# GpSimd takes the short operations behind every four expert dots and behind their tanh

## The chip, the cores and the metric

The kernel runs on one core of a Trainium2 chip. The metric is the device time of one execution in microseconds; the comparison rests on medians of several runs. The core's engines are TensorE (PE, with its weight load PEld), VectorE (DVE), ScalarE (ACT), GpSimd (POOL) and SyncE (SP, which here only issues DMAs). Each runs its own instructions in order and waits on semaphores for the others.

## The reference, cut to what matters

Input x is 2048 rows of 512 floats. After a layer norm, the output is the sum of x, an attention and a layer of many small experts:

```python
xn = _layernorm(x, axis=-1)
return x + _A_ref(xn, ...) + _B_ref(xn, ...)
# _A_ref: 32 heads of 16, one shared k and v: softmax(q k^T / 4) v, then @ wo
# _B_ref, for every row and each of 32 heads:
#   s1, s2 = q1 @ k1^T, q2 @ k2^T          64 scores each
#   the best 2 of each, the best 2 of their 4 sums -> 2 experts of 4096, gates g = softmax
act = _gelu(jnp.einsum("nd,nhkd->nhk", xf, u[top_e]))
out = jnp.einsum("nhk,nhk,nhkd->nd", g, act, v[top_e])
```

The gelu is the tanh form: half of a (1 + tanh(0.798 a + 0.0357 a^3)).

## The kernel before, in words

The 2048 rows are 16 tiles of 128, in four groups of four. Two ways of computing the experts stand side by side.

**Gathered experts** serve the first eight tiles (`ph` 0 and 1), for the first of the heads' chosen experts at a time: a slot is one expert for each of a tile's 128 rows. There are 512 slots. For every slot, `gather` (L969) has POOL fetch 128 rows of u and v side by side with an indirect DMA into one of 12 buffers; `dot` (L981) multiplies the u half with xn and sums it on DVE into one column of a 128x4 tile `act`; `add` (L1014) adds the v half, times its weight, to the tile's total on DVE and so frees the buffer. Between dot and add, four slots together (a group, 128 in all) pass through short operations on 128x4 tiles: L997 and L998 form the argument of the tanh (`q`, then `y`), L999 multiplies the dots with the gates (`ga`), ACT takes the tanh (`tanh`, L1002, row L1004), and L1011 in `weigh` makes the weight `w = (th + 1) ga`. All four but the tanh are on DVE.

**Dense experts** serve the other eight tiles, in two stages (`dense`, L656): gates are spread over all 4096 experts with one-hot matmuls (`pg`, L815), then u and v run as plain matmuls in blocks of 128 experts (`pact` L733, `pout` L861), with DVE splitting operands (L698, L919), multiplying gates (L904, L907, L924) and adding totals (L864).

Ahead of both, `item` (L512) scores one tile against a share of the heads with 12 matmuls into a PSUM buffer `psc` (L531); DVE finds the best eight and their places (L544, L546); after every four items `batch` (L563) does the choice of the best two, with part of it on POOL (L590 to L606 for the gathered, L590 to L638 for the dense experts).

Attention runs through all of this in 256 double steps (`att_steps`, L1142): scores (`sc`, L326), exp on ACT (`pt`, L329), times v (`pv`, L340). One PE item of other work fills each step: `fill` runs scores or dense work up to a planned time.

The order of the instructions on every engine is written out by hand (`manual_schedule`, L1248): each engine runs what the program emits for it, in the order of emission. In a step, `mid` (L1264) emits first the tanhs of the groups whose dots stand in earlier steps, then this step's dots, with `weigh` ahead of the last dot, and then `go` (L1294): one add, one operation of `CHAIN`, one of `BEHIND` in turn, and up to four gathers. `CHAIN` is the list into which `dot` puts L997 to L999, so that these lie between adds; in the one-hot stages (`dense_on` 2) the whole list runs right after the dots. The three PSUM buffers of the tag `x` serve psc, pact, pout, pg and the small transposes in turn; DVE or ACT frees them. The tiles of the short operations rotate over three or four buffers.

Of the kernel before, what the change touches and what calls it, by code (L numbers as in the profile page):

```python
# [11 lines left out]
F32 = mybir.dt.float32  # L12
# [5 lines left out]
AF = mybir.ActivationFunctionType  # L18
OP = mybir.AluOpType
# [4 lines left out]
P = 128  # L24
# [15 lines left out]
SB = 4  # L40
# [7 lines left out]
C_IN = 0.7978845608028654  # L48
C_CUB = 0.044715 * C_IN
# [6 lines left out]
def tile_kernel(ctx, tc, x, wq, wkv, wo, wqT, kT, uv, ub, vb, out):  # L56
    nc = tc.nc
# [6 lines left out]
    small = pool("small", bufs=2)  # L64
# [381 lines left out]
    def experts_out(t):  # L446
        acc, last = ACC[t], t // GT == QB[3]
        assert last or t in DONE_A
        store(lambda: nc.sync.dma_start(d_part[t] if last else out[t * P:(t + 1) * P, :], acc))
        LIVE.discard(t)  # L450
# [513 lines left out]
             for h in range(NEG // 2) for k in range(2) for i in range(2)]  # L964
    NSL = len(slots)
    UV, WT, ACTS, TH, GA = {}, {}, {}, {}, {}
    CHAIN = []

    def gather(m):  # L969
        ph, c, ti, s = slots[m]  # L970
# [10 lines left out]
    def dot(m):  # L981
        ph, c, ti, s = slots[m]
        n, i = divmod(m, SB)
        if i == 0:
            ACTS[n] = small.tile([P, SB], F32, name="act", bufs=3)
        a = ACTS[n]
        u = UV[m][:, :D]
        nc.vector.tensor_tensor_reduce(u, u, XN[TPH * ph + ti], scale=1.0, scalar=0.0,  # L988
                                       op0=OP.mult, op1=OP.add, accum_out=a[:, i:i + 1])
        if i == SB - 1:  # L990
            q = small.tile([P, SB], F32, name="gq", bufs=3)
            y = small.tile([P, SB], F32, name="gy", bufs=3)
            ga = small.tile([P, SB], F32, name="ga", bufs=4)
            gg = G[ph, c][:, ti - 1:ti + 1, s // 2, :].rearrange("p t k -> p k t")
            pairs = lambda v: v.rearrange("p (k t) -> p k t", t=2)
            stt = nc.vector.scalar_tensor_tensor
            CHAIN.append(lambda: stt(q, a, C_CUB, a, op0=OP.mult, op1=OP.mult))  # L997
            CHAIN.append(lambda: stt(y, q, C_IN, a, op0=OP.add, op1=OP.mult))  # L998
            CHAIN.append(lambda: nc.vector.tensor_tensor(out=pairs(ga), in0=pairs(a), in1=gg, op=OP.mult))  # L999
            TH[n], GA[n] = y, ga  # L1000

    def tanh(n):  # L1002
        th = small.tile([P, SB], F32, name="gth", bufs=3)
        nc.scalar.activation(th, TH[n], AF.Tanh)  # L1004
        TH[n] = th

    def weigh(n):
        if n not in WT and n < a_ready[0] // SB:
            ga, th = GA.pop(n), TH.pop(n)
            w = small.tile([P, SB], F32, name="w", bufs=3)  # L1010
            nc.vector.scalar_tensor_tensor(w, th, 1.0, ga, op0=OP.add, op1=OP.mult)  # L1011
            WT[n] = w

    def add(m):  # L1014
        ph, c, ti, s = slots[m]
        n, i = divmod(m, SB)
        weigh(n)
        if i == SB - 1:
            weigh(n + 1)
        w = WT[n]  # L1020
        acc = ACC[TPH * ph + ti]
        v = UV.pop(m)[:, D:]
        nc.vector.scalar_tensor_tensor(acc, v, w[:, i:i + 1], acc, op0=OP.mult, op1=OP.add)  # L1023
        if c == NC - 1 and s == NEG - 1:
            OUTS.append(TPH * ph + ti)


    g_next, d_next, a_next, a_ready = [0], [0], [0], [0]

    def gathers(most):  # L1030
        while g_next[0] < NSL and g_next[0] < a_next[0] + NGB - lent[0] and most > 0:
            gather(g_next[0])
            g_next[0] += 1
            most -= 1

    def dots(to):
        while d_next[0] < min(to, NSL):
            dot(d_next[0])
            d_next[0] += 1

    def adds(most):
        while a_next[0] < a_ready[0] and most > 0:
            add(a_next[0])
            a_next[0] += 1
            most -= 1

    def tanhs(to):
        while a_ready[0] + SB <= to:
            tanh(a_ready[0] // SB)
            a_ready[0] += SB  # L1050
# [8 lines left out]
    def run(fns):  # L1059
        todo = fns[:]  # L1060
        fns.clear()
        for fn in todo:
            fn()
# [6 lines left out]
    def flush():  # L1070
        posts()
        for _ in range(2):
            for fns in (ON_ACT, LAST, LATER, BEHIND):
                run(fns)
            ON_ACT.extend(LATER_ACT)
            LATER_ACT.clear()
        run(ON_ACT)
        run(BEHIND)
# [40 lines left out]
    dense_on, quiet = [0], [0]  # L1119
# [3 lines left out]
    def run_scores(until=None, key=None):  # L1123
        while (until is not None and spent[0] < until) or (key is not None and key not in IDX):
            posts()
            try:
                cost = next(sgen)
            except StopIteration:
                spent[0] = 1e9
                posts()  # L1130
                return
            if cost is None:

                if key is None:
                    return
                continue
            spent[0] += cost

    STEPS = 512


    def att_steps(d, mid, fill):  # L1142
        i = 2 * d
        run(STORES)
# [66 lines left out]
    for i in range(2):  # L1211
        for k in range(2):
            w = start.tile([P, 2, 512], F32R, name="wqs", tag="wqs", bufs=4)
# [34 lines left out]
    with tc.manual_schedule(engines={E_.PE, E_.Activation, E_.DVE, E_.Pool, E_.SP}):  # L1248
        done0 = spent[0]
        half = STEPS // 2  # L1250
        pos, since = 0.0, half
        for d in range(half + 24):


            if dense_on[0] != 0:
                since = d
            if dense_on[0] == 1:
                pos += 2.6 if d < half * 3 // 4 else max(0.0, NSL - pos) / max(half - 3 - d, 1)
            else:
                pos += (2.1 if len(IDX) < NC * TPH else 2.3 if 0 <= d - since < 12 else 1.75, 0, 1.4, 1.5, 0.5)[dense_on[0]]  # L1260

            todo = max(min(int(pos + 0.001), g_next[0]) - d_next[0], 0)

            def mid():  # L1264
                post = POST[:]
                POST.clear()
                for act, _ in post:
                    act()
                tanhs(d_next[0])
                run(ON_ACT)  # L1270
                ON_ACT.extend(LATER_ACT)
                LATER_ACT.clear()
                run(LAST)
                LAST.extend(LATER)
                LATER.clear()
                rest = BEHIND[:]
                BEHIND.clear()

                dots(d_next[0] + todo - 1)
                if a_ready[0] > a_next[0]:  # L1280
                    weigh(a_next[0] // SB)
                dots(d_next[0] + 1 if todo > 0 else 0)
                for _, fn in post:
                    fn()
                sums = min(a_ready[0] - a_next[0], max(todo, 3) if d < half else 4)
                if dense_on[0] > 2:
                    sums = min(sums, 2)
                if quiet[0] > 0:
                    quiet[0] -= 1
                    sums = 0  # L1290
                if dense_on[0] == 2:
                    run(CHAIN)

                def go():  # L1294
                    n = sums
                    while rest or CHAIN or n > 0:
                        if n > 0:
                            adds(1)
                            n -= 1
                        elif not rest:  # L1300
                            run(CHAIN)
                        if CHAIN:
                            CHAIN.pop(0)()
                        if rest:
                            rest.pop(0)()
                    gathers(4)

                    for _ in range(1 if d < half - 4 else NT):
                        if OUTS:
                            experts_out(OUTS.pop(0))  # L1310

                if dense_on[0] == 2:
                    POST_FILL.append(go)
                else:
                    go()

            aim = done0 + (FILL - done0) * (d + 1) / half if d < half else 1e6

            def fill():
                run_scores(until=min(aim, spent[0] + MOST))  # L1320
                run(POST_FILL)

            att_steps(d, mid, fill)
        flush()
        run(STORES)
        while a_next[0] < NSL:
            dots(NSL)
            run(CHAIN)
            tanhs(d_next[0])
            adds(SB)  # L1330
            run(STORES)
            gathers(NGB)
        assert not OUTS
        run(STORES)


def build(nc, tc, args):
    tile_kernel(tc, *args)
# [33 lines left out]
```

## Time and profile before

| | |
|---|---|
| median of 3 runs | 1926.75 us (1924.97 to 1935.35) |
| the profiled execution | 1925.78 us |
| its span, first to last instruction | 1924.1 us |
| mean granted clock of TensorE | 0.981 |
| instructions | 34929 |

All rows are of that one profiled execution. A group's row gives the line of the code, the engine, the operation, the tile written and the tiles read, shapes and count; then the busy time in us, the mean of one in ns, and the idle time of the engine just before, with what ended it. A row of the timeline gives the start in us, the length in us, and the same names. A row of the waits gives who waited for whom, the total in us, how many times, and the longest. Rows by stage give the stage, its length and the busy time of each engine with the number of instructions, then the granted clock, the DMA share and GB/s.

### The profile page before, as it was taken

The page shows a single profiled execution, that of the slowest core. Times are in us where ns is not written, and L with a number is a line of the kernel's source. Part 1 is how long each engine was busy: PE and PEld are TensorE (multiplying, and loading weights), DVE is VectorE, ACT ScalarE, POOL GpSimd, SP SyncE. Part 2 cuts the span into 40 slices and gives each one's busy share as a digit, 9 for nine tenths or more (in the row PEclk, how much of TensorE's full clock was granted, in tenths as well). Part 3 has the DMA queues.
Part 4 walks back from the last instruction along what each step waited for, and adds up shares of the span by engine and source line. Part 5 has one row for each costly group of instructions (what it writes and reads, how often), then busy time and mean ns, then how long its engine had stood idle before and what let it go on. Part 6 is the DMA issues. An engine that isn't in the chain of part 4 may idle for free.

```text
span 1924.1 us, 34929 instructions
## 1 busy us (share of the span) xinstructions
PE 1863.8 (97%) x10990; PEld 991.8 (52%) x10990; DVE 1634.0 (85%) x6381; ACT 1294.2 (67%) x1803; POOL 700.8 (36%) x920
## 2 busy tenths in 40 slices
PE   6979999999999999999999999999999999999998
PEld 3634444555555554555555554555555455555553
DVE  6627787989998977999999897899988779999994
ACT  3346666655557887787877555555578777888873
POOL 1203334434452223343444444355422134344430
PEclk9989999999999899999999999999988899999999
DMA  7857789787773778888999987876736778899882
GB/s 274 315 186 278 266 272 301 279 296 251 249 246 122 233 240 249 253 288 270 287 300 309 362 287 237 280 256 220 242 105 220 249 215 292 271 284 286 282 277 84
DMA packets 234395, 491.13 MB, mean 255 GB/s; under 512 B 93396, under 2 KB 93396, under 8 KB 234204
## 3 DMA queue, kind: packets, MB, share of 16 engines
q0 software_dynamic: 73728, 268.47, 42.0%
q1 hardware_dynamic: 159240, 219.56, 34.9%
q8 instruction: 88, 1.44, 0.3%
q10 hardware_dynamic: 1236, 0.82, 0.1%
q14 instruction: 103, 0.84, 0.1%
HBM read 427.41 MB, written 56.07 MB: 251 GB/s over the span
## 4 chain that ended last, share of the span: by engine, by line
PE 85%; DMA 3%; ACT 3%; DVE 1%; issue 1%; SPq 0%; DVEq 0%; ACTq 0%
PE pv L340 24%; PE psc L531 18%; PE sc L326 17%; PE pact L733 9%; PE pout L861 9%; PE pg L815 3%; PE pwo L433 2%; ACT pt L329 2%; PE pw L486 1%; DMA wqt<-in_wqT_dram 1%; DMA dinv<-rc 1%; DMA wk<-dw 1%; PE pwt L493 0%; PE pwl L408 0%; DMA qa<-dqh 0%
## 5 line engine op out<-in xcount | busy, mean ns | idle before, releaser
L329 ACT ACTIVATE pt<-sc 128x1024 f32<-128x1024 f32 x1024 | 993.7, 1026 | 461.9 <-PE sc L326 460.5
L976 POOL DMA_INDIRECT g<-in_uv_dram,idx x512 | 556.8, 1087 | 1002.0 <-DVE xa L1023 531.0
L340 PE MATMUL pv<-pt,vaug 128*32 128x512 f32 x4096 | 516.4, 623 | 0.0
L531 PE MATMUL psc<-wk,xt 128*128 128x512 f32 x1536 | 388.7, 401 | 4.1 <-DVE wk L496 3.5
L326 PE MATMUL sc<-qa,kaug 64*128 64x512 f32 x2048 | 384.2, 451 | 8.6 <-ACT pt L329 8.4
L1023 DVE SCALAR_TENSOR_TENSOR xa<-g,w,xa 128x512 f32<-128x512 f32 x512 | 371.7, 744 | 0.1
L988 DVE CUSTOM_DVE_ANT_0 g<-g,xa 128x512 f32<-128x512 f32 x512 | 335.5, 681 | 7.4 <-DMA g<-in_uv_dram,idx 7.4
L531 PEld LDWEIGHTS psc<-wk,xt 128*128 128x128 f32 x1536 | 277.9, 188 | 107.7 <-issue 37.5
L326 PEld LDWEIGHTS sc<-qa,kaug 64*128 64x128 f32 x2048 | 155.9, 185 | 329.3 <-ACT pt L329 218.8
L340 PEld LDWEIGHTS pv<-pt,vaug 128*32 128x32 f32 x4096 | 109.6, 111 | 257.0 <-issue 255.4
L546 DVE FIND_INDEX8 i<-m,psc 128x8 uint32<-128x64 f32 x1024 | 206.3, 220 | 0.0
L733 PE MATMUL pact<-xt,wk 128*128 128x512 f32 x768 | 195.9, 400 | 0.0
L861 PE MATMUL pout<-wk,wd 128*128 128x512 f32 x768 | 194.8, 401 | 0.2 <-DVE wd L919 0.2
L544 DVE MAX8 m<-psc 128x8 f32<-128x64 f32 x1024 | 146.2, 213 | 41.1 <-PE psc L531 40.3
L861 PEld LDWEIGHTS pout<-wk,wd 128*128 128x128 f32 x768 | 140.8, 188 | 47.3 <-DVE act L988 5.5
L733 PEld LDWEIGHTS pact<-xt,wk 128*128 128x128 f32 x768 | 139.4, 188 | 48.5 <-issue 17.5
L698 DVE TENSOR_TENSOR wk<-rw,wk 128x512 fp32r<-128x512 f32 x128 | 84.8, 683 | 9.7 <-ACT wk L697 9.7
L864 DVE TENSOR_TENSOR da<-da,pout 128x512 f32<-128x512 f32 x128 | 82.8, 679 | 10.1 <-PE pout L861 10.0
L783 DVE TENSOR_TENSOR oh<-oh 128x2048 f16<-128x2048 f16 x64 | 78.0, 1219 | 0.8 <-ACT oh L759 0.6
L815 PEld LDWEIGHTS <-oh 128*128 128x128 f16 x1024 | 68.4, 162 | 13.8 <-issue 6.4
L1011 DVE SCALAR_TENSOR_TENSOR w<-gth,ga 128x4 f32<-128x4 f32 x128 | 20.4, 159 | 64.5 <-ACT gth L1004 64.0
L815 PE MATMUL pg<-oh 128*128 128x32 f16 x1024 | 73.5, 247 | 0.6 <-DVE oh L786 0.5
(159 smaller groups left out, 1411.1 us busy)
## 6 DMA issues: line engine op xcount, KB each, us to landing
wk<-dw SPq DMA_DIRECT2D x96, 512.0 KB
wqt<-in_wqT_dram SPq DMA_DIRECT2D x32, 512.0 KB
dw<-wk SPq DMA_DIRECT2D x32, 512.0 KB
rw<-in_ub_dram SPq DMA_DIRECT2D x64, 256.0 KB
rw<-in_vb_dram SPq DMA_DIRECT2D x64, 256.0 KB
gy<-dg SPq DMA_DIRECT2D x64, 256.0 KB
qa<-dqh SPq DMA_DIRECT2D x128, 64.0 KB
g<-in_uv_dram,idx POOLq DMA_INDIRECT x512, 6.0
```

The lines of the kernel that those rows point to most:

```text
L326: nc.tensor.matmul(p[:, b, :], kaug[o:o + 64, kc * P:(kc + 1) * P], QA[u][o:o + 64, i, :], start=True, stop=True)
L329: nc.scalar.activation(pt, p, AF.Exp, scale=SCALE)
L340: nc.tensor.matmul(PV[u][32 * j:32 * j + 32, :], vaug[:, kc, :], pt[:, b, :], start=kc == 0, stop=kc == 15)
L531: nc.tensor.matmul(p, XT[g][k][:, a, j * P:(j + 1) * P], WC[n_][k][:, bb, :], start=n == 0, stop=n == 11)
L544: nc.vector.max(m8[:, jb, s, :], p[:, s * E:(s + 1) * E])
L546: nc.vector.max_index(i8[:, jb, s, :], m8[:, jb, s, :], p[:, s * E:(s + 1) * E])
L733: nc.tensor.matmul(p, us[:, a, k * P:(k + 1) * P], XT[DG][k][:, c, :], start=n == 0, stop=n == 11)
L815: nc.tensor.matmul(p[:, i * NB:(i + 1) * NB], oa[:, :, i], ob[:, :, i], start=True, stop=True)
L861: nc.tensor.matmul(p, wd[0][:, a, j * P:(j + 1) * P], vs[:, c, :], start=n == 0, stop=n == 5)
L976: nc.gpsimd.indirect_dma_start(out=gt, out_offset=None, in_=uv, in_offset=bass.IndirectOffsetOnAxis(ap=IDX[ph, c, ti][:, s:s + 1], axis=0))
L988: nc.vector.tensor_tensor_reduce(u, u, XN[TPH * ph + ti], scale=1.0, scalar=0.0, op0=OP.mult, op1=OP.add, accum_out=a[:, i:i + 1])
L1023: nc.vector.scalar_tensor_tensor(acc, v, w[:, i:i + 1], acc, op0=OP.mult, op1=OP.add)
```

## The change

The short operations move from DVE to POOL, the list `CHAIN` and the function `weigh` go. POOL has no operation here that does two steps with two tensors, so the argument of the tanh takes three operations instead of two, and the weight two instead of one: six instead of four. The first four are emitted right where the group's fourth dot is; the last two right behind the group's tanh, at the start of the step's work, ahead of its dots. The order of PE's, ACT's and SP's instructions is the same as before; DVE's is the same without the four. On POOL, a step's order is now: weights of the groups whose tanh the step has, the four operations of a group that the step's dots complete, gathers, and a batch's share if one falls there. Of the 32 batches, 16 are followed on POOL directly by two weight operations and 13 by the four chain operations. Adds on DVE now wait for POOL, and so does the tanh on ACT.

```diff
     def dot(m):
...
-            stt = nc.vector.scalar_tensor_tensor
-            CHAIN.append(lambda: stt(q, a, C_CUB, a, op0=OP.mult, op1=OP.mult))
-            CHAIN.append(lambda: stt(y, q, C_IN, a, op0=OP.add, op1=OP.mult))
-            CHAIN.append(lambda: nc.vector.tensor_tensor(out=pairs(ga), in0=pairs(a), in1=gg, op=OP.mult))
+            V = nc.gpsimd
+            V.tensor_mul(q, a, a)
+            V.tensor_scalar(q, q, C_CUB, C_IN, op0=OP.mult, op1=OP.add)
+            V.tensor_mul(y, q, a)
+            V.tensor_tensor(out=pairs(ga), in0=pairs(a), in1=gg, op=OP.mult)
             TH[n], GA[n] = y, ga
 
     def tanh(n):
         th = small.tile([P, SB], F32, name="gth", bufs=3)
-        nc.scalar.activation(th, TH[n], AF.Tanh)
-        TH[n] = th
-
-    def weigh(n):
-        if n not in WT and n < a_ready[0] // SB:
-            ga, th = GA.pop(n), TH.pop(n)
-            w = small.tile([P, SB], F32, name="w", bufs=3)
-            nc.vector.scalar_tensor_tensor(w, th, 1.0, ga, op0=OP.add, op1=OP.mult)
-            WT[n] = w
+        nc.scalar.activation(th, TH.pop(n), AF.Tanh)
+        ga = GA.pop(n)
+        w = small.tile([P, SB], F32, name="w", bufs=3)
+        nc.gpsimd.tensor_mul(w, th, ga)
+        nc.gpsimd.tensor_add(w, w, ga)
+        WT[n] = w
...
                 dots(d_next[0] + todo - 1)
-                if a_ready[0] > a_next[0]:
-                    weigh(a_next[0] // SB)
                 dots(d_next[0] + 1 if todo > 0 else 0)
...
-                if dense_on[0] == 2:
-                    run(CHAIN)
-
                 def go():
                     n = sums
-                    while rest or CHAIN or n > 0:
+                    while rest or n > 0:
                         if n > 0:
                             adds(1)
                             n -= 1
-                        elif not rest:
-                            run(CHAIN)
-                        if CHAIN:
-                            CHAIN.pop(0)()
                         if rest:
                             rest.pop(0)()
                     gathers(4)
```

More of the change, by code (lines that the diff above doesn't have):

```diff
@@ L966, in tile_kernel @@
     UV, WT, ACTS, TH, GA = {}, {}, {}, {}, {}
-    CHAIN = []
     def gather(m):
@@ L1016, in add @@
         n, i = divmod(m, SB)
-        weigh(n)
-        if i == SB - 1:
-            weigh(n + 1)
         w = WT[n]
@@ L1327, in tile_kernel @@
             dots(NSL)
-            run(CHAIN)
             tanhs(d_next[0])
```

## The prediction

> **What bounds the kernel now.** I read the page's busy shares first, then the chain that ended last, then the busy time by stage, and last the waits of PE.
>
> ```profile
> PE 1863.8 (97%) x10990; PEld 991.8 (52%) x10990; DVE 1634.0 (85%) x6381; ACT 1294.2 (67%) x1803; POOL 700.8 (36%) x920
> PE 85%; DMA 3%; ACT 3%; DVE 1%; issue 1%; SPq 0%; DVEq 0%; ACTq 0%
> ```
>
> PE is busy for 97% of the span and makes 85% of the chain; DVE, from which the change takes work, makes 1%. An average can hide a stage that DVE sets, so I cut the span by the kernel's stages: the two dense ones (760 to 1060 and 1540 to 1895) and the second stretch of scores and gathers (1060 to 1402). Columns: length, then busy us of PE, PEld, DVE, ACT, POOL.
>
> ```profile
> 760.00:1060.00 300.00, 299.39 (x1694) 165.23 (x1696) 284.99 (x666) 237.76 (x339) 124.68 (x110) 1.00 0.90 285
> 1060.00:1402.00 342.00, 341.14 (x1919) 183.41 (x1911) 307.65 (x1874) 198.53 (x242) 156.65 (x256) 1.00 0.78 266
> 1540.00:1895.00 355.00, 354.70 (x1993) 190.84 (x1986) 325.15 (x756) 277.40 (x391) 137.36 (x122) 1.00 0.85 265
> ```
>
> PE idles 0.61, 0.86 and 0.30 us there. DVE idles 15.0 us, 34.4 us and 29.9 us: it is second, near the bound only in the dense stages. What PE waited for from DVE after 200 us, where the changed code runs (columns: total us, times, longest):
>
> ```profile
> PE pwt L493 <- DVE i L546: 2.3, 1, 2.3
> PE psc L531 <- DVE wk L496: 1.9, 3, 0.7
> ```
>
> Together 4.2 us; two smaller ones follow further down, and one on L415 at the end stands behind a DMA. So about 5 us is all that a lighter DVE can give to PE by these rows.
>
> **What leaves DVE.** Four small operations for every four dots:
>
> ```profile
> L1011 DVE SCALAR_TENSOR_TENSOR w<-gth,ga 128x4 f32<-128x4 f32 x128 | 20.4, 159 | 64.5 <-ACT gth L1004 64.0
> L999 DVE TENSOR_TENSOR ga<-act,gg 128x4 f32<-128x4 f32 x128 | 20.2, 158 | 0.0
> L998 DVE SCALAR_TENSOR_TENSOR gy<-gq,act 128x4 f32<-128x4 f32 x128 | 20.2, 158 | 1.6
> L997 DVE SCALAR_TENSOR_TENSOR gq<-act 128x4 f32<-128x4 f32 x128 | 20.1, 157 | 0.4
> ```
>
> By durations that is 80.9 us. But operations overlap on DVE. The timeline of one step with a batch of scores in it:
>
> ```profile
> 502.94 3.70 PE L531 MATMUL psc<-wk,xt 128*128 128x512 f32 x15
> ...
> 503.97 0.08 DVE L988 DVE_READ_ACCUMULATOR2_ANT act<- 128x1 f32 x1
> ...
> 508.13 0.31 POOL L590 CAST fi<-i 128x64 f32<-128x64 uint32 x1 [2.20 <-DVE i L546]
> ...
> 508.68 0.22 POOL L629 TENSOR_TENSOR e<-fi 128x16 f32<-128x16 f32 x1
> ...
> 508.97 0.67 POOL L630 TENSOR_TENSOR e<-e,cond 128x16 f32<-128x16 f32 x1
> 509.00 0.21 ACT L1004 ACTIVATE gth<-gy 128x4 f32<-128x4 f32 x1
> ...
> 509.48 0.17 DVE L1011 SCALAR_TENSOR_TENSOR w<-gth,ga 128x4 f32<-128x4 f32 x1
> 509.58 0.68 DVE L988 CUSTOM_DVE_ANT_0 g<-g,xa 128x512 f32<-128x512 f32 x1
> ...
> 509.72 0.63 POOL L631 TENSOR_TENSOR ii<-e,fi 128x16 f32<-128x16 f32 x1
> ...
> 510.19 2.07 DVE L1023 SCALAR_TENSOR_TENSOR xa<-g,w,xa 128x512 f32<-128x512 f32 x3
> ...
> 514.09 0.46 POOL L638 TENSOR_TENSOR da<-hi,ii 128x32 f32<-128x32 f32 x2
> ```
>
> The weight operation at 509.48 lets the next dot start at 509.58: it costs 0.10 us of DVE's time, not 0.17. I take 0.1 us for each of the 512, so 51 us (bounds 51 and 80.9). To PE this is worth between 0 and the 5 us above; I take 0, since none of those waits ends on one of the four operations.
>
> **What comes to POOL.** Six 128x4 operations for every four dots. The nearest rows are its own small ones: a two-input operation takes 0.22 us when DVE runs small things (508.68) and 0.63 to 0.67 us when DVE runs a dot or an add (508.97, 509.72). Starts of dependent ones lie 0.29 us apart (508.68 to 508.97) or 0.75 us (508.97 to 509.72). So four operations behind the dots take 1.2 to 3.0 us, of which the tanh needs the first three (0.9 to 2.3), and the two behind the tanh 0.6 to 1.5. For 128 groups: 128 x 1.8 = 230 us to 128 x 4.5 = 576 us. I take the middle, some 400: in most places dots or adds run beside. It fits:
>
> ```profile
> L976 POOL DMA_INDIRECT g<-in_uv_dram,idx x512 | 556.8, 1087 | 1002.0 <-DVE xa L1023 531.0 <-DVE gq L997 237.2 <-DVE gy L998 68.6
> ```
>
> POOL sat idle 1002 us in front of gathers, waiting for adds to free their buffers. So it is latency in POOL's order that counts, not its load.
>
> **The chain in front of tanh.** It waits on POOL for the fourth dot. Now the fourth dot's result is there at 504.05 and its tanh starts at 509.00: 4.95 us later. POOL's three operations take at most 2.3, so ACT doesn't wait, unless POOL is in the middle of a batch of top-two work (508.13 to 514.55, 6.4 us). Then tanh can be late by 2 us or so and the exp behind it too; PE has the 15 matmuls of 3.70 us (502.94) to run before it needs that exp. I take 0 for PE, bounds 0 to 3 us.
>
> **The weights behind tanh.** Now DVE has w 0.27 us after the tanh in the quoted step (509.21 to 509.48), with a dot between w and the add. In the new order w stands on POOL in front of the chain and the gathers of the same step, but behind the gathers of the step before and, 16 times of 32, straight behind a batch. Queued behind a waiting add on DVE are the step's other adds, the splits, and the maxima of the next scores; PE waits for these only when its three score buffers are full.
> - Behind a batch: in the quoted step the batch ends at 514.55, w would come at 515.2 and the adds, now at 510.19, 5.0 us late. With DVE stopped, the batch runs at its free speed (four operations of some 0.4 us less each): 3.4 us. I estimate that half of the 16 places lose little, their group's add coming later anyway; eight by 3.4 is 27 us of DVE in both score stages together, against 34.4 us idle in the second alone. Cover for PE are the two other buffers, 12 matmuls or 2.96 us each (3.70/15 a matmul), and the attention between. I take 1 us for PE; bounds are 0, and, with one buffer free and the batch at its slow speed, 8 x (5.0 - 2.96) = 16.
> - In the dense stages there are no batches. Groups there, by the count of tanhs, and what DVE waits for them:
>
> ```profile
> 760.00:1060.00 300.00, 5.61 (x27) 1.00 0.90 285
> 1540.00:1895.00 355.00, 6.64 (x32) 1.00 0.85 265
> ```
>
> ```profile
> DVE w L1011 <- ACT gth L1004: 6.1, 5, 3.0
> ```
>
> ```profile
> 808.67 0.21 ACT L1004 ACTIVATE gth<-gy 128x4 f32<-128x4 f32 x1
> ...
> 809.95 0.74 DVE L1023 SCALAR_TENSOR_TENSOR xa<-g,w,xa 128x512 f32<-128x512 f32 x1
> ```
>
> In 5 of 27 groups of the first stage DVE waits for the tanh. In the example w is due 0.97 us after the tanh (808.88 to 809.95, less 0.1 for the operation that goes), and POOL needs 0.6 to 1.5: late by 0 to 0.5. I take 0.4 us a group as a mean, with gathers in front of some. That is 59 x 0.4 = 24 us of DVE against a relief of 59 x 4 x 0.1 = 24 us and 44.9 us idle. DVE stays second; single tiles may hold PE for a moment. I take 1 us, bounds 0 and the rival below.
>
> **The sum** is 0 + 0 + 1 + 1 = 2 us on the profiled execution's own 1925.78 us (span 1924.1): **1928 us**. The median of the three runs shown is 1926.75, 1.0 above that execution.
>
> **A rule of the Trainium skill.** POOL's operation takes three times as long beside a dot, and ends with it. The Trainium skill, "Advanced Engine Details and Errata", section "VectorE Performance Modes" (Mode Summary), says that GpSimd and two-port vector instructions block each other, and section "Miscellaneous Facts" (GPSIMD Details) counts vector instructions with two SBUF inputs among those that conflict. The trace agrees for POOL. For DVE, the three adds at 510.19 take 2.07 us with POOL operations beside; here are three with none:
>
> ```profile
> 639.90 2.07 DVE L1023 SCALAR_TENSOR_TENSOR xa<-g,w,xa 128x512 f32<-128x512 f32 x3
> ```
>
> DVE isn't held. By that page's word "eachother" it would be, which is the second rival below.
>
> **Rivals.**
> 1. *Late weights make DVE the bound of the dense stages (slower).* Every add group waits for two contended operations on POOL, behind four of the chain and a gather of 1.09 us. It decides from where the mean stall passes (24 + 44.9) / 59 = 1.17 us a group. At 1.6 us, about the contended pair alone with no cover, it adds 59 x 1.6 - 69 = 25 us: 1951. For it: only 5 to 8 of 100 us of DVE are free there, and POOL is in order. Against: the tanh comes early enough in most groups, and a waiting DVE makes POOL fast again. Chance 0.24.
> 2. *POOL's operations hold DVE* for their own 0.22 us each. That is 59 x 6 x 0.22 = 78 us of DVE in the dense stages: 9 us beyond the 69 that relief and idle time give, 54 if the idle time falls in the wrong places; in the middle some 30 us, 1956. Against: the equal 2.07 us. Chance 0.04.
> 3. *DVE was holding PE unseen* (ends of matmuls are modelled), and its relief comes through: the 24 us of the dense stages in half: 1914. Against: PE's waits on DVE are about 5 us. Chance 0.05.
>
> **How the numbers follow.** The forecast, PE goes on setting the time, has 0.67 and its own range of 1921 (all 5 gained) to 1936 (3 for the tanh, half of the 16 behind batches); what goes beyond I count with rival 1. The range of 8 in 10 takes in most of rival 1: 1920 to 1950; outside are rival 3, the far half of rival 1 and part of rival 2. Over 0.5%, 9.6 us, about what a measurement of this kernel can tell from no change: faster 0.05 (rival 3), slower 0.28 (rivals 1 and 2), same 0.67.
>
> **What the profile after would show.** PE still idle under 2 us in each dense stage; DVE's four groups gone and its busy time 50 to 81 us lower; POOL's six lines at 0.2 to 0.7 us each, 170 to 510 us busy in all; DVE waits named on POOL's w, some 30 to 60 us in total, the longest behind a batch; hardly any ACT wait on POOL's y; adds still at 0.74 us. I am wrong if PE shows new waits on psc, pact or pout tiles that DVE frees, if adds or dots grow longer, or if ACT's tanh waits for y in many steps.

## The result, and the profile after

The changed kernel takes 1942.3 us (median of 9 runs, 1933.25 to 1944.19) against 1926.75 us before (now also of 9 runs, 1920.58 to 1935.35): **slower, 1.0071 times the time before, 95% interval 1.0048 to 1.0093**. This ratio and all that follow are of the means of the runs; the medians give 1.0081. In a second round on another chip the ratio was 1.0098 (1.0076 to 1.0119). The time lies in the range given, but the case called likeliest (within 0.5%) did not come.

The profiled execution took 1942.0 us, span 1940.3, granted clock 0.978. Its page, busy shares and the chain that ended last:

```profile
PE 1868.8 (96%) x10990; PEld 994.6 (51%) x10990; DVE 1590.5 (82%) x5869; ACT 1293.9 (67%) x1803; POOL 977.8 (50%) x1688
PE 76%; DVE 9%; POOL 3%; ACT 2%; issue 1%; DMA 1%; SPq 0%; DVEq 0%; POOLq 0%; ACTq 0%
```

DVE lost 43.5 us of work and POOL took 277 us, yet DVE now makes 9% of the chain (1% before) and POOL 3% (none before). Work left DVE, and waiting came instead. The groups on POOL and DVE that show it (busy us, mean ns, then the idle time in front and what ended it):

```profile
L975 POOL DMA_INDIRECT g<-in_uv_dram,idx x512 | 553.8, 1082 | 310.9 <-DVE xa L1017 157.4
L1017 DVE SCALAR_TENSOR_TENSOR xa<-g,w,xa 128x512 f32<-128x512 f32 x512 | 372.0, 748 | 100.2 <-POOL w L1008 98.7
L987 DVE CUSTOM_DVE_ANT_0 g<-g,xa 128x512 f32<-128x512 f32 x512 | 332.5, 687 | 20.8 <-DMA g<-in_uv_dram,idx 20.8
L996 POOL TENSOR_TENSOR gq<-act 128x4 f32<-128x4 f32 x128 | 63.9, 499 | 255.9 <-DVE act L987 255.5
```

```profile
L1007 POOL TENSOR_TENSOR w<-gth,ga 128x4 f32<-128x4 f32 x128 | 38.7, 302 | 199.9 <-ACT gth L1004 191.3 <-ACT ex L583 7.6
```

Read them by their idle columns. Before, POOL idled 1002 us in front of gathers, that is, it stood ready when a buffer came free. Now it idles 311 us there and 256 + 200 us in front of the chain and the weights, waiting for dots and tanh **with gathers queued behind**. From the add that frees a buffer to the gather that fills it again, the median over all gathers grew from 0.46 to 1.49 us. And DVE, which never waited for POOL's `w`, waits 98.7 us for it.

Most of this is hidden by PE, as the prediction said. The dense stages after, less the end of the first (columns as in the tables by stage before):

```profile
776.00:1066.00 290.00, 289.48 (x1633) 160.19 (x1632) 268.33 (x537) 230.83 (x329) 196.58 (x263) 1.00 0.88 276
1556.00:1911.00 355.00, 354.79 (x2000) 190.65 (x1988) 316.42 (x629) 277.60 (x392) 215.57 (x313) 1.00 0.84 266
```

PE idles 0.5 and 0.2 us there. At the end of the first dense stage, which these rows leave out, it idles 4.3 us (1066 to 1090); that is place 3 below. So I looked for the places where the time is lost. The 256 double steps of the attention are the same work in both kernels, and each has four exp operations (L329), so the start of every fourth exp is a ruler: I laid the after trace's step lengths beside those of before. Outside the first 430 us and the two one-hot stages, the steps are equal to within 0.3 us, except at four places. The places, with what they lost in the profiled execution and in a second profiled execution of the changed kernel:

| place (us in the trace before) | double steps | first | second |
|---|---|---|---|
| 1: at 556, score stage | 58, 59 | 1.60 | 2.18 |
| 2: at 597, into the first one-hot stage | 64 | 6.34 | 6.40 |
| 3: 1052 to 1081, dense stage into scores | 132 to 135 | 5.51 | 6.57 |
| 4: 1365 to 1415, score stage, into the second one-hot stage | 177 to 183 | 2.77 | 3.19 |
| sum | | 16.2 | 18.3 |

The exps that begin step 64, before and after, as an example of the ruler. A row "x2" is two exps, so the first and third rows of each begin a step:

```profile
597.05 1.94 ACT L329 ACTIVATE pt<-sc 128x1024 f32<-128x1024 f32 x2
599.67 1.93 ACT L329 ACTIVATE pt<-sc 128x1024 f32<-128x1024 f32 x2
605.17 1.04 ACT L329 ACTIVATE pt<-sc 128x1024 f32<-128x1024 f32 x1
```

```profile
600.42 1.94 ACT L329 ACTIVATE pt<-sc 128x1024 f32<-128x1024 f32 x2
603.04 1.93 ACT L329 ACTIVATE pt<-sc 128x1024 f32<-128x1024 f32 x2
614.89 1.96 ACT L329 ACTIVATE pt<-sc 128x1024 f32<-128x1024 f32 x2
```

8.12 us before, 14.47 after. The four places sum to 16.2 us, the difference of the spans. The rest nearly cancels: the first exp came 2.6 us later; the steps from there to 430 us were together 0.8 shorter; the one-hot stages were 5.6 longer and 7.0 shorter. A second profile of the *unchanged* kernel differs from the first by 2.8, 1.4, 5.5 and -8.2 us there and by at most 0.5 us at the four places, so these differences can't be told from what executions of one kernel differ by. In the one-hot stages the clock decides: over stretches of 10 us it lies between 0.68 and 1.0, and by the clock record of the trace it falls to half, for 3.4 us at a time, 5 times in the first and 11 times in the second stage, against 8 and 6 times in the second profile of that kernel. Each time costs half of 3.4 us, so that makes 5 us more and 8.5 us less, close to the 5.5 and -8.2.

**Place 2.** POOL and DVE after, from the last batch before the one-hot stage on. The first row is a batch's first operation, the second its last, then the weights; the third fence is DVE's add:

```profile
600.97 0.31 POOL L590 CAST fi<-i 128x64 f32<-128x64 uint32 x1 [4.37 <-DVE i L546]
...
604.75 0.46 POOL L638 TENSOR_TENSOR da<-hi,ii 128x32 f32<-128x32 f32 x2
605.17 0.20 POOL L1007 TENSOR_TENSOR w<-gth,ga 128x4 f32<-128x4 f32 x1
```

```profile
592.53 0.26 POOL L590 CAST fi<-i 128x64 f32<-128x64 uint32 x1 [9.44 <-DVE i L546]
```

```profile
605.68 1.41 DVE L1017 SCALAR_TENSOR_TENSOR xa<-g,w,xa 128x512 f32<-128x512 f32 x2 [4.00 <-POOL w L1008]
```

The second fence is the same batch before. It began 4.52 us ahead of its step's first exp (592.53 against 597.05); now it begins 0.55 us behind (600.97 against 600.42): late by 5.1 us. It waits for DVE's index search (L546), and DVE had stood still for weights, 2.42 us at 565.18 (behind a late tanh) and 3.70 at 583.31 (behind the batch ahead of this one). Then the add waits 4.00 us once more, since the weights stand behind this batch too. And here PE has nothing else: the one-hot stage starts from the batch's own result. PE's waits after (from 200 us on, rows that matter):

```profile
PE sc L326 <- ACT pt L329: 8.6, 19, 1.0
PE pout L861 <- DVE wd L919: 4.6, 3, 4.0
...
PE ptd L758 <- DVE da L649: 1.8, 1, 1.8
PE ptd L758 <- DVE gy L746: 1.8, 1, 1.8
PE ptd L758 <- POOL da L638: 1.3, 1, 1.3
```

The three on `ptd`, the transposes that begin the one-hot stage, are place 2; the 4.0 on `pout` is place 3.

**Place 3.** The end of the dense stage; POOL after, with the waits that stand in front of a gather, then the same gather before and the add that freed its buffer, then the freeing add and the dot after:

```profile
1056.49 0.58 POOL L996 TENSOR_TENSOR gq<-act 128x4 f32<-128x4 f32 x1 [2.28 <-DVE act L987]
...
1062.50 0.20 POOL L1007 TENSOR_TENSOR w<-gth,ga 128x4 f32<-128x4 f32 x1 [2.40 <-ACT gth L1004]
...
1065.24 1.33 POOL L975 DMA_INDIRECT g<-in_uv_dram,idx  x1 [0.15 <-issue]
```

```profile
1038.46 1.57 POOL L976 DMA_INDIRECT g<-in_uv_dram,idx  x1 [0.30 <-issue]
```

```profile
1037.26 0.74 DVE L1023 SCALAR_TENSOR_TENSOR xa<-g,w,xa 128x512 f32<-128x512 f32 x1
```

```profile
1052.65 0.75 DVE L1017 SCALAR_TENSOR_TENSOR xa<-g,w,xa 128x512 f32<-128x512 f32 x1
...
1074.43 0.69 DVE L987 CUSTOM_DVE_ANT_0 g<-g,xa 128x512 f32<-128x512 f32 x1 [5.09 <-DMA g<-in_uv_dram,idx]
```

The buffer was free at 1053.40 (end of the add at 1052.65); the gather was issued at 1065.24, 11.8 us later. Before, it followed its add (1037.26 and 0.74) by 0.46 us. Its dot waits 5.09 us, and behind the dot stands the split that `pout` needs: PE waits 4.0.

The loss is larger than the wait, because the clock drops behind it: the granted clock is 0.65 from 1082 to 1086 us and 0.93 from 1086 to 1090, by the clock record half from 1083.2 to 1086.6, which costs 1.7 us more. At place 2 it is half from 608.7 to 615.6, twice as long as before (609.6 to 613.0). The other runs below bear this out: PE waits 2.4 us or more on `pout` at place 3 in eight of the thirteen profiles, and seven of these have 3.4 to 10.2 us at half clock there (the chain back on DVE has none); of the five without the wait none has. That the wait brings the drop was not tested by itself. So the losses in the table below can differ by some us at the same wait.

**Places 1 and 4.** The chain behind a batch, and the tanh that waits for it:

```profile
561.12 0.47 POOL L638 TENSOR_TENSOR da<-hi,ii 128x32 f32<-128x32 f32 x2
561.55 0.65 POOL L996 TENSOR_TENSOR gq<-act 128x4 f32<-128x4 f32 x1
```

```profile
563.12 0.21 ACT L1004 ACTIVATE gth<-gy 128x4 f32<-128x4 f32 x1 [3.91 <-POOL gy L998]
```

The exp behind the tanh is late, and PE's next scores with it. At place 4 two tanhs wait 3.21 and 2.72 us.

### The profile page after: what moved, and what is told of

It is laid out like the page before. It is cut to its first block, busy times and chain, and to the rows that moved or that the text cites. A ratio compares the mean times of both kernels' runs of the same rounds, so it can differ in the third digit from the quotient of the medians.

```text
span 1940.3 us, 35218 instructions
## 1 busy us (share of the span) xinstructions
PE 1868.8 (96%) x10990; PEld 994.6 (51%) x10990; DVE 1590.5 (82%) x5869; ACT 1293.9 (67%) x1803; POOL 977.8 (50%) x1688
## 4 chain that ended last, share of the span: by engine, by line
PE 76%; DVE 9%; POOL 3%; ACT 2%; issue 1%; DMA 1%; SPq 0%; DVEq 0%; POOLq 0%; ACTq 0%
PE pv L340 22%; PE sc L326 15%; PE psc L531 13%; PE pout L861 9%; PE pact L733 9%; PE pg L815 3%; DVE i L546 3%; PE pwo L433 2%; DVE xa L1017 2%; DVE m L544 2%; ACT pt L329 1%; PE pw L486 1%; DVE g L987 1%; DMA g<-in_uv_dram,idx 0%; PE pwt L493 0%
## 5 line engine op out<-in xcount | busy, mean ns | idle before, releaser
L329 ACT ACTIVATE pt<-sc 128x1024 f32<-128x1024 f32 x1024 | 992.9, 1026 | 456.4 <-PE sc L326 454.9
L975 POOL DMA_INDIRECT g<-in_uv_dram,idx x512 | 553.8, 1082 | 310.9 <-DVE xa L1017 157.4
L1017 DVE SCALAR_TENSOR_TENSOR xa<-g,w,xa 128x512 f32<-128x512 f32 x512 | 372.0, 748 | 100.2 <-POOL w L1008 98.7
L546 DVE FIND_INDEX8 i<-m,psc 128x8 uint32<-128x64 f32 x1024 | 207.6, 231 | 0.0
L996 POOL TENSOR_TENSOR gq<-act 128x4 f32<-128x4 f32 x128 | 63.9, 499 | 255.9 <-DVE act L987 255.5
L1007 POOL TENSOR_TENSOR w<-gth,ga 128x4 f32<-128x4 f32 x128 | 38.7, 302 | 199.9 <-ACT gth L1004 191.3
L546 DVE MATCH_VALUE_LOAD i<-m,psc 128x8 f32 x1024 | 81.3, 79 | 0.0
```

What stands on the lines that cost most here:

```text
L329: nc.scalar.activation(pt, p, AF.Exp, scale=SCALE)
L546: nc.vector.max_index(i8[:, jb, s, :], m8[:, jb, s, :], p[:, s * E:(s + 1) * E])
L975: nc.gpsimd.indirect_dma_start(out=gt, out_offset=None, in_=uv, in_offset=bass.IndirectOffsetOnAxis(ap=IDX[ph, c, ti][:, s:s + 1], axis=0))
```

## The theories

*Theory 1, the order of POOL's queue.* What stands behind a wait or a batch on POOL is late: weights (then DVE's adds, searches and the next batch), the chain (then tanh and exp), gathers (then dots). Only places without other work for PE show it. *Theory 2, the load:* POOL's operations hold DVE in proportion to their number. *Theory 3:* the clock in the one-hot stages fell out badly. Each run is compared with the kernel before on its own chip, by ratio. In this table are the places' losses in one profiled execution of each, against the first profile of before, in us (at place 3 for step 133 alone, where the change has 6.19; step 135 is left out, since in profiles without the loss PE can wait there for a load of `wk`, 1.3 us in two of them and 0.8 in before again):

| kernel | 1 | 2 | 3 | 4 | ratio, 95% interval |
|---|---|---|---|---|---|
| the change | 1.60 | 6.34 | 6.19 | 2.77 | 1.0071 (1.0048 to 1.0093) |
| the change again | 2.18 | 6.40 | 7.22 | 3.19 | 1.0098 (1.0076 to 1.0119) |
| weights back on DVE | 0.00 | 0.00 | 4.01 | 0.00 | 1.0035 (1.0017 to 1.0053) |
| chain back on DVE | 0.00 | 7.10 | 3.07 | 1.24 | 1.0079 (1.0052 to 1.0107) |
| batch put off | 0.00 | -0.01 | 6.26 | 0.47 | 1.0009 (0.9988 to 1.0029) |
| six operations without waits | 0.00 | 0.01 | 0.04 | 0.04 | 1.0018 (1.0004 to 1.0033) |
| two waits alone | 0.00 | 0.01 | 6.48 | -0.01 | 1.0027 (1.0009 to 1.0046) |
| gathers first, batch put off, weights on DVE | 0.00 | 0.00 | -0.06 | -0.01 | 1.0053 (1.0030 to 1.0076) |
| all six behind, batch put off | 0.00 | 0.00 | 5.60 | 0.18 | 1.0054 (1.0034 to 1.0074) |
| no short operations | 0.00 | -0.01 | -0.05 | -0.01 | 0.9974 (0.9954 to 0.9994) |
| twelve without waits | 0.00 | 0.00 | 7.89 | -0.02 | 1.0227 (1.0197 to 1.0258) |
| before again | 0.00 | 0.00 | 0.00 | -0.03 | 0.9995 (0.9977 to 1.0012) |

## The experiments

**Weights back on DVE.** The chain's four operations stay on POOL where the change has them; `weigh` and its calls come back.

```diff
-        nc.gpsimd.tensor_mul(w, th, ga)
-        nc.gpsimd.tensor_add(w, w, ga)
...
+    def weigh(n):
...
+            nc.vector.scalar_tensor_tensor(w, th, 1.0, ga, op0=OP.add, op1=OP.mult)
```

> The chain's four operations stay on GpSimd, the weights are one operation of VectorE again. Theory 1 (the order of GpSimd's queue, four places): the place at the first one-hot stage, where adds waited for weights behind a batch (6.3 us), goes; the two places where tanh waits for a chain behind a batch (1.6 and 2.4 us) stay; the place where gathers came late (5.5 us) stays or halves, since the chain still stands in front of the gathers and the weights don't. In all 4 to 10 us over the kernel before: 1931 to 1937. Theory 2 (GpSimd's load as such holds VectorE, by the number of operations): four of six operations are left, two thirds of 15.6 us: 1937, spread over all stages. Theory 3 (throttling in the one-hot stages fell out badly in the profiled execution): as after, 1942, or as before, without relation to the edit.

1.0035. Place 2 is gone, place 3 has 4.0, as expected. But places 1 and 4 are gone too, which I had not expected: I had blamed the chain behind the batch for them. The batch that place 2 turned on begins in time again:

```profile
600.12 0.26 POOL L590 CAST fi<-i 128x64 f32<-128x64 uint32 x1 [6.02 <-DVE i L546]
```

Its step's first exp starts at 604.64, so it is 4.52 us ahead, to the hundredth as before. At place 1 the batch is 5.14 us ahead of its step (before 4.92, the change 1.09), and the tanh behind it waits 0.20 us instead of 3.91. So the late weights make the *batch* late, and the late batch makes the chain late: places 1, 2 and 4 need the weights on POOL.

**Chain back on DVE.** The counterpart: only the weights' two operations on POOL, `CHAIN` as before. Against the kernel before:

```diff
-            nc.vector.scalar_tensor_tensor(w, th, 1.0, ga, op0=OP.add, op1=OP.mult)
...
+        nc.gpsimd.tensor_mul(w, th, ga)
+        nc.gpsimd.tensor_add(w, w, ga)
```

> The chain's three operations are VectorE's again, only the two operations of the weights stay on GpSimd. Theory 1: the place at the first one-hot stage (weights behind a batch) stays, 6 us; both places where tanh waited for the chain (1.6 and 2.4 us) go; the late gathers (5.5 us) stay or halve, since the weights' wait for tanh still stands in front of them and the wait for the dots doesn't. In all 6 to 12 us: 1933 to 1939. Theory 2: two of six operations, a third of 15.6 us: 1932, spread over all stages. Theory 3: no relation to the edit.

1.0079, above the 6 to 12 us expected (1.003 to 1.006). Place 2 is there in full (7.1, and 1.1 more in the step ahead of it; its batch begins 1.1 us behind its step's exp), place 1 is gone, since no tanh waits for POOL (it takes both, weights that delay the batch and a chain behind it), and place 4 is 1.2. Place 3 is 3.1: PE waits 3.0 us instead of 4.0, and no drop of the clock follows. With two operations this loses about as much as the change with six: theory 2, by number, falls. (The mean granted clock of these runs was 0.975 against 0.979 for the kernel before on that chip, so the ratio may hold more than the places; the places alone come to 11.8 us, twice the 5 us of theory 2.)

**Batch put off.** All six on POOL; a batch's operations on POOL, but the first, are collected (`Later` puts each into the list `PUT_OFF`) and emitted behind the next step's weights and chain.

```diff
+        run(PUT_OFF)
-        G_ = nc.gpsimd
-        G_.tensor_copy(fi, i8[:, :, :, 0:2])
+        nc.gpsimd.tensor_copy(fi, i8[:, :, :, 0:2])
+        G_ = Later(nc.gpsimd) if late[0] is not None else nc.gpsimd
...
                 dots(d_next[0] + 1 if todo > 0 else 0)
+                run(PUT_OFF)
```

> All six operations stay on GpSimd; a batch's operations on GpSimd (all but the first, a cast) are put behind the next step's weights and chain in its queue. Theory 1: no weights and no chain stand behind a batch, so three of the four places go (1.6, 6.3 and 2.4 us); the gathers that come late behind chain and weights stay, 5.5 us: 1930 to 1935. Against it stands what a later batch costs by itself where TensorE waits for it, at the start of a one-hot stage: up to 2 us each. Theory 2: the load is the same, 1942. Theory 3: no relation.

1.0009, less than expected (1.002 to 1.004): the same work on the same engine, in another order, and three of the four places are gone; the time can't be told from that of the kernel before. POOL at place 2, where the weights now pass the batch:

```profile
594.71 0.32 POOL L600 CAST fi<-i 128x64 f32<-128x64 uint32 x1 [4.43 <-DVE i L546]
595.00 0.20 POOL L1020 TENSOR_TENSOR w<-gth,ga 128x4 f32<-128x4 f32 x1
...
595.42 0.20 POOL L571 COPY ii<-fi 128x16 f32<-128x16 f32 x1
```

The profiled execution still has place 3 (6.3 us), and near 970 us a wait of DVE of 6.1 us for a load of gates, twice the longest such wait in any other profile; at 1936.48 us it was slower than the median of its 12 runs, 1934.50. By place 3 alone I would expect 1.003, just above the interval; why the runs show less stays open.

**Six operations without waits.** The kernel before, with the change's number of operations added on POOL behind every fourth dot, on a tile of their own.

```diff
+            x0, x1 = idle[:, :SB], idle[:, SB:]
+            V.tensor_mul(x1, x0, x0)
...
+            V.tensor_add(x1, x1, x0)
```

> The kernel before, with six operations on 128x4 added on GpSimd behind every fourth dot that work on a tile of their own: no wait for dots or tanh and nothing that waits for them but GpSimd's own queue (the four short operations are VectorE's, as before). Theory 1: the load alone costs nothing, 0 to 2 us: 1926 to 1929. Theory 2: it costs as much as the change: 1942. If it lies between, the load has a part in it.

1.0018, and nothing at any place. DVE's wait for gathers (from 200 us on; 16.6 us in the change) is that of before, 2.8:

```profile
DVE g L990 <- DMA g<-in_uv_dram,idx: 2.8, 3, 1.1
```

So six more operations delay nothing that PE sees. They do use up slack: the gather that is late at place 3 is issued 6.4 us behind the add that frees its buffer, against 0.46 before and 11.8 in the change, and its dot still finds it landed. A small part, some 3.5 us, is left without a place in the order.

**Two waits alone.** The kernel before, with one POOL operation that reads the dots and one that reads the tanh; nobody reads them.

```diff
+            nc.gpsimd.tensor_mul(idle[:, :SB], a, a)
...
+        nc.gpsimd.tensor_mul(idle[:, SB:], th, th)
```

> The kernel before with two operations on 128x4 added on GpSimd behind every fourth dot, one that reads the dots and one that reads their tanh, where the change has its chain and its weights; nothing reads what they write, so neither tanh nor the adds wait for GpSimd. It adds the two waits to GpSimd's queue and hardly any work. Theory 1: only the gathers behind them come late: 4 to 7 us at 1060 to 1090 us, nothing at the other three places, ratio 1.002 to 1.005. If the late gathers came from the work on GpSimd and not from its waits: nothing there, ratio 0.999 to 1.001.

1.0027; place 3 has 6.5 us and the others nothing. POOL there:

```profile
1054.77 0.52 POOL L1003 TENSOR_TENSOR idle<-act 128x4 f32<-128x4 f32 x1 [3.00 <-DVE act L990]
...
1060.68 0.20 POOL L1009 TENSOR_TENSOR idle<-gth 128x4 f32<-128x4 f32 x1 [4.02 <-ACT gth L1007]
...
1061.62 1.29 POOL L978 DMA_INDIRECT g<-in_uv_dram,idx  x1
```

This gather is issued 10.0 us behind its add, and PE waits 3.8 us on `pout`. Not all of that is gathers: ahead of the split DVE waits 1.74 us for a load of the softmax's sums, 0.45 for POOL to have read the dots, and 1.75 for a gather. Still, two operations that wait do what six that don't wait do not: POOL's waits are enough for place 3, and DVE's short operations, all back here, have no part in it.

**Gathers first.** The chain's four operations on POOL behind the step's gathers, the weights on DVE, the batch put off.

```diff
+            CHAIN.append(lambda: V.tensor_mul(q, a, a))
...
                     gathers(4)
+                    run(CHAIN)
```

> The chain's four operations on GpSimd but behind the step's gathers in its queue, the weights one operation of VectorE, a batch's operations behind both. Every order that theory 1 blames is taken away, while four of the six operations stay on GpSimd. Theory 1: none of the four places is left (0 us each; above all nothing at 1060 to 1090 us, where the chain before the gathers left 4.0 us): ratio 0.999 to 1.002. Theory 2 (load): 1.0035 or more, as with the chain alone in its old order.

All four places are gone, and yet 1.0053: the total missed, and it is what theory 2 expected. Only the trace tells the two apart. Two new ones came, 2.0 us each, at steps 235 and 236, and smaller ones. ACT there, and its total wait for the chain:

```profile
1770.85 0.21 ACT L1018 ACTIVATE gth<-gy 128x4 f32<-128x4 f32 x1 [2.28 <-POOL gy L1012]
```

```profile
ACT gth L1018 <- POOL gy L1012: 31.3, 29, 3.3
```

31.3 us in 29 waits, against 13.8 in 8 in the change. The chain now stands behind gathers, which wait for adds; the tanh is late, and ACT's exp behind it. The loss moved to what I had put last in POOL's queue: 2.5 us in the first dense stage and 5.8 from the second on. By these rows that is theory 1 again, but not the "nothing left" that I derived from it.

**All six behind.** As the last, with the weights on POOL too. Against the change, beside the batch put off:

```diff
-            V.tensor_mul(q, a, a)
...
+            CHAIN.append(lambda: V.tensor_mul(q, a, a))
...
                     gathers(4)
+                    run(CHAIN)
```

> All six operations on GpSimd as in the change, the chain behind the step's gathers and a batch's operations behind weights and chain; only the weights' two operations, which wait for tanh, still stand in front of the gathers. Theory 1: the places of the batch are gone; at 1060 to 1090 us some 3 us are left, as where the weights alone stood there, instead of 6.2: ratio 1.000 to 1.003. Theory 2: the load is that of the change: 1.007.

1.0054 instead of at most 1.003, between the two theories. At place 3 PE waits 3.0 us, as the expectation had it, but 6.8 us at half clock stand behind the wait (1070.3 to 1077.1), which makes 5.6. And tanh waits as in the run before: both losses stand side by side. It is still less than the change, 1.0098 on that chip.

**No short operations.** The kernel before without all four; tanh is taken of the dots and is the weight, so gates and polynomial are left out.

```diff
-            TH[n], GA[n] = y, ga
+            TH[n] = a
...
-        nc.scalar.activation(th, TH[n], AF.Tanh)
-        TH[n] = th
+        nc.scalar.activation(th, TH.pop(n), AF.Tanh)
+        WT[n] = th
```

> The kernel before without the four short operations: tanh is taken of the dots themselves and its result is the weight, so the gates and the polynomial are left out of the result; nothing is added on GpSimd. It shows what the relief of VectorE is worth by itself. Theory 1: TensorE sets the pace and the relief is worth nothing: ratio 0.999 to 1.001 to the kernel before. The rival (VectorE held TensorE unseen): 4 to 14 us faster, ratio 0.993 to 0.998.

0.9974: relief is worth about 5 us, half a per cent at most. That is not the nothing of theory 1; it lies at the upper end of what the rival expected. But the rival's place, VectorE holding TensorE, isn't in the trace: the four places and the dense stages are as before to 0.2 us, and the profile differs up to step 57 (+2.3 us) and in the one-hot stages (-1.5, -5.0), where two executions of the kernel before differ by more. Where the 5 us come from stays open.

**Twelve without waits.** The six of above twice.

```diff
             V.tensor_add(x1, x1, x0)
+            V.tensor_mul(x1, x0, x0)
...
+            V.tensor_add(x1, x1, x0)
```

> Twelve operations on GpSimd that wait for nothing and that nothing waits for, twice the six of the earlier run, which took 1.0018 times the kernel before at a mean granted clock lower by 0.002. If GpSimd's load has a price of its own through the granted clock: twice that, ratio 1.003 to 1.005 and a clock lower by 0.003 to 0.004, and no place in the order of the work where it is lost. If the 1.0018 was chance: 0.999 to 1.002 again.

1.0227, far beyond either expectation. The load isn't free at twice the dose. The wait for gathers in front of the dots, by lines:

```profile
L990 DVE CUSTOM_DVE_ANT_0 g<-g,xa 128x512 f32<-128x512 f32 x512 | 337.6, 682 | 57.3 <-DMA g<-in_uv_dram,idx 52.1 <-issue 5.1
```

It is 7.4 us before and 52.1 here; a dot takes 682 ns, as before (681). Place 3 has 7.9 us here though POOL waits for nothing new, and more such places appear in the dense stages (8.4 us at step 245, where a dot waits 6.2 us for its gather). So the added work does not slow DVE's dots; it makes gathers late. Theory 2 as stated, DVE held in proportion to POOL's operations, falls, but load alone can bring the late gathers of theory 1: none that PE sees at six operations, many at twelve.

**Before again**, and **the change again**, both unedited.

> The kernel before against itself, for a second profile of it: ratio 0.999 to 1.001. All theories: no difference of the two profiles at the four places (within 0.3 us); what differs in the first 200 us and in the two one-hot stages is what executions of one kernel differ by.

> The changed kernel once more, for a second profile and a ratio on this chip. Theory 1: the same four places with the same sizes (1.6, 6.3, 5.5 to 6.2 and 2.4 us, within 1 us where no transfer decides; the late gathers may differ, as their landing does) and a ratio of 1.005 to 1.009. Theory 3: the places move or go, since they were one execution's throttling.

0.9995 and 1.0098, the second just above the range expected. The four places come back within 1.1 us in the change and are absent in the kernel before; the one-hot stages differ as freely between executions of one kernel as between the two kernels. Theory 3 falls. No version with all of the work in it ran faster than the kernel before; the batch put off can't be told from it.

## Why the prediction was right and wrong

The sum was 2 us, 1928; measured are 15.6 by the medians. That the range to 1950 holds the time is partly luck: it was drawn so wide for rival 1, late weights in the dense stages, and the loss came at other places.

- **PE sets the pace, relief of DVE gives 0 to 5 us:** the size is right, but I took 0. Without the short operations the kernel gains 5 us, though not by waits of PE that went; with them on POOL nothing of it was seen.
- **DVE's cost of the four operations**, 51 us (50 to 81 less busy time expected): 43.5, and 40.0 between the second profiles; below the bounds, 0.08 us an operation instead of 0.10.
- **POOL's price**, 0.2 to 0.7 us an operation, 230 to 576 us, 400 taken: the six rows are 305 us busy, near the lower end (POOL as a whole 277 more, since the batches' rows became shorter). The chain's first, L996, has a mean of 499 ns, the weights 302 and 318. The remark drawn from it, that latency in POOL's order counts and not its load, was right; I then followed it for `w` and `y` only. (That load costs nothing holds at six operations and not at twelve.)
- **The step that failed is one that isn't there:** gathers. The quoted row of 1002 us of POOL's idle time shows gathers waiting for buffers, ready to go at once. Putting two waits for DVE and ACT ahead of them takes that readiness away. No term had it; it cost 5.5 to 6.6 us at place 3, and the two waits alone reproduce 6.5. One of the prediction's own signs of being wrong came true here in part: PE waits 4.6 us on `pout`, 0.2 before, though for DVE's splits and not for a tile that DVE frees.
- **"The weights behind a batch", 1 us taken, bounds 0 to 16, was mis-sized.** The stall was right: of the 16 places behind a batch, DVE waits 3.4 to 4.0 us at eight and less than 2 at the others, as estimated (eight by 3.4); at 515.27 and at 537.23 it is 3.39 us, and there PE hid it as said. In all DVE waited 98.7 us for `w`, against the 30 to 60 expected. Wrong was to count cover by score buffers in mid-stage only. At the end of the stage the one-hot matmuls need the batch itself, and the stalls had made that batch 5.1 us late. Place 2 costs 6.3; with places 1 and 4, which also go when the weights go back, 10.7 us, within the bounds.

```profile
515.27 1.42 DVE L1017 SCALAR_TENSOR_TENSOR xa<-g,w,xa 128x512 f32<-128x512 f32 x2 [3.39 <-POOL w L1008]
```

- **"The chain in front of tanh", 0 taken, bounds 0 to 3:** ACT waited 8 times, 13.8 us in all, so "hardly any" was wrong, and two places show it, 4.4 us together, above the bound. By itself, with the chain alone on POOL, it cost nothing at either; it costs when weights have made the batch late.
- **Late weights in the dense stages, 1 us:** right up to the end of the first one, where place 3 lies: DVE waits 7.4 and 10.0 us for `w` there, against the 24 in the sum, and PE idles 0.5 and 0.2 us. Rival 1's mechanism, weights that make DVE the bound, did not come. Its chance bore some of the truth (slower, by POOL's order), not its place.
- **POOL holding DVE (rival 2), and the rule of the Trainium skill**, "Advanced Engine Details and Errata", "VectorE Performance Modes" (Mode Summary), by which the two would block each other: an add takes 748 ns against 744 before and a dot 687 against 681, with 768 more operations on POOL; with 1536 more, in twelve without waits, they take 743 and 682. The trace shows POOL slowed and DVE hardly or not. Twelve operations cost much, but by late gathers.
- **DVE holding PE unseen (rival 3):** not at a place that the traces show.

## What to carry to other kernels

An in-order engine that mostly waits is not a free engine: its idle time may be what lets its next instruction start at once. Before moving work there, list what stands behind each new wait, above all DMA issues, and look for cover not only within a stage but at its end, where the bound engine needs the late thing itself. To find a loss of under 1%, lay a repeated instruction of the bound thread, here every fourth exp, of two traces side by side: it puts the loss at a few places, and a second trace of the same kernel shows which of them are only the execution's.

## What the runs showed of the hardware that was not expected

POOL's spare time runs out abruptly: six added operations per group that wait for nothing cost a ratio of 1.0018, twelve 1.0227.

A wait of PE can cost more than its length. At place 3, waits of 2.4 to 4.7 us came with 3.4 to 10.2 us at half of the clock in seven profiles of eight, and in the five profiles without the wait the clock did not drop there.

The mean granted clock also differed between kernels: over the runs of one comparison it was 0.9774 with the six operations without waits against 0.9792 for the kernel before on that chip, 0.9708 with the twelve against 0.9788, 0.9825 without the short operations against 0.9808. It does not go with the number of operations on POOL: it was 0.975 against 0.979 with two (chain back on DVE), but 0.979 against 0.979 with four (weights back on DVE) and 0.981 against 0.981 with six (all six behind). Among the runs of the kernel before, a clock lower by 0.001 went with 1.0 to 1.4 us more. By that the clock would be worth some 2.6 us of the 3.5 us of the six without waits and some 1.7 us of the 5 us without the short operations; this is an estimate, and what lowers the clock stays open.
